# Threshold attention before two feed-forward layers: threshold sums per head on GpSimd, value products spread over five steps, a shorter warm-up

## The chip, the cores and the metric

The kernel runs on one core of a Trainium2 chip. The metric is the device time of one execution in microseconds (us). Engines are named as the profile names them: PE (TensorE) with its weight loads PEld, DVE (VectorE), ACT (ScalarE), POOL (GpSimd) and SP (SyncE, which issues DMAs).

## What is computed

Attention over 4 batches of 8 heads, 576 positions and 64 values per head, keeps of each row of scores only those within tau of the row's maximum; its output goes through a gated layer (width 1536) and a second one (width 2048), all in float32:

```
scores = scale * np.matmul(q, k.transpose(0, 1, 3, 2))
thresh = np.max(scores, axis=-1, keepdims=True) - tau
scores = np.where(scores >= thresh, scores, -1000000000.0)
scores = scores - np.max(scores, axis=-1, keepdims=True)
attn = np.exp(scores)
attn = attn / (np.sum(attn, axis=-1, keepdims=True) + 1e-09)
out = np.matmul(attn, v)
x = (sigmoid(x @ w_gate) * (x @ w_val)) @ w_out
x = g(x @ w_in) @ w_out2      # g: 0, a quarter parabola, then the identity
```

## The kernel before

Attention takes two heads (e = 0 and 1) at a time: 16 pairs p, each in five steps u = 0 to 4 of 128 rows of queries (step 4 holds the last 64 rows of both heads in one tile). The order is written by hand: `attention` counts t over 80 steps, and each engine takes what the steps issue to it strictly in that order. In step t:

- PE forms the scores of step t (`scores`, L235 and L239) in `wa` and `wb`, transposes the weights of step t-1 (`turns`, L280 and L281), and does a part of the products with the values (`attend`, L304), which `rounds` (L365) assigns to steps. A pair's products are cut into round 0 (query rows of steps 0 and 1) and round 1 (steps 2 to 4); each has five chunks c of keys, 0 to 3 from the tile `r`, 4 from the tile `rl`, with two products (one per head) for a chunk. Rounds of pair p run in steps 3, 4, 6 and 7 counted from its first; 5 and more lie in the next pair.
- DVE takes, head by head, the scaled negated scores and their row minimum (`maxima`, L248); POOL then adds tau for both heads in one instruction (L251); ACT takes the exponentials (`exponents`, L258); DVE multiplies by the mask and sums the rows (`masks`, L266, which reads the tiles `s` and `ex` and POOL's sum); POOL copies the rest of the keys (`lt`, L273).
- ACT copies the transposes of step t-1 from PSUM (`copies`, L286 to L296) and, when a round ends, its result (`drain`, L314).
- Once a pair, in step 0 of the next, DVE adds 1e-9 to the row sums and inverts them (`denom`, L318 and L319); they are transposed (L384), go to DRAM and back spread over the partitions (`sum_rows`, `spread`), and POOL multiplies the result by them in step 4 (`normalise`, L335).

Beside this, from step 12 on, a generator `background` puts one DVE or ACT operation of the conversion of the first weights behind the masks of a step, and later steps split the first inputs and weights of the next layer there. The feed-forward layers follow, bound by PE. Before the first scores, `warm` (L354) issues products of the identity with itself that no one reads.

Of the kernel before, what the change touches and what calls it, by code (L numbers as in the profile page):

```python
# [14 lines left out]
ALU = mybir.AluOpType  # L15
# [14 lines left out]
def kernel(  # L30
# [17 lines left out]
    nc = tc.nc  # L48
# [3 lines left out]
    NP, _, S = q.shape  # L52
# [7 lines left out]
    nf, R = divmod(S, P)  # L60
# [17 lines left out]
    tau_b = const.tile([P, 1], F32, name="tau_b")  # L78
# [8 lines left out]
    sums = [const.tile([P, 2 * nf + 1], F32, name=f"sum_{i}") for i in range(2)]  # L87
# [99 lines left out]
    def attention():  # L187
# [14 lines left out]
        U = nf + 1  # L202
# [8 lines left out]
        def load(p):  # L211
            t = qkp.tile([P, 2, S], F32, tag="qk", name="qk")
            nc.sync.dma_start(out=t[:, 0], in_=q[p])
            nc.sync.dma_start(out=t[:, 1], in_=k[p])
            qk[p] = t
# [9 lines left out]
        def corner(p):  # L225
            for e in range(2):
                es = slice(e * R, e * R + R)
                nc.gpsimd.tensor_copy(corners[p % 2][es, es], qk[p][es, 0, nf * P :])

        def scores(p, u):  # L230
            t = qk[p]
            for s in range(2):
                c = slice(s * HS, s * HS + HS)
                if u == nf:
                    nc.tensor.matmul(wa[:, s, :HS], corners[p % 2], t[:, 1, c], start=True, stop=True)  # L235
                    continue
                for e, w in enumerate((wa, wb)):
                    es = slice(e * D, e * D + D)
                    nc.tensor.matmul(  # L239
                        w[:, s, :HS], t[es, 0, u * P : u * P + P], t[es, 1, c], start=True, stop=True  # L240
                    )

        def maxima(p, u):

            t = sp.tile([P, 2, 2, HS], F32, tag="s", name="s")
            mx = mxs[u % 2]
            for e, w in enumerate((wa, wb)[: 1 if u == nf else 2]):
                nc.vector.tensor_scalar(  # L248
                    t[:, e], w[:, :, :HS], nscale, None, op0=ALU.mult, op1=ALU.min, accum_out=mx[:, 0, e : e + 1]
                )  # L250
            nc.gpsimd.tensor_scalar(mx[:, 1], mx[:, 0], tau_b, None, op0=ALU.add)  # L251
            st[p, u] = t, mx

        def exponents(p, u):
            t, mx = st[p, u]
            ex = pe_.tile([P, 2, 2, HS], F32, tag="ex", name="ex")
            for e in range(1 if u == nf else 2):
                nc.scalar.activation(ex[:, e], t[:, e], AF.Exp, scale=-1.0, bias=mx[:, 0, e : e + 1])  # L258
            st[p, u] = t, mx, ex

        def masks(p, u):
            t, mx, ex = st.pop((p, u))
            pr = pt[p, u] = pp.tile([P, 2, S], F32, tag="p", name="p")
            for e in range(1 if u == nf else 2):
                c = 2 * nf if u == nf else e * nf + u
                nc.vector.scalar_tensor_tensor(  # L266
                    pr[:, e], t[:, e].rearrange("p a b -> p (a b)"), mx[:, 1, e : e + 1],
                    ex[:, e].rearrange("p a b -> p (a b)"), op0=ALU.is_le, op1=ALU.mult,
                    accum_out=sums[p % 2][:, c : c + 1],
                )  # L270
            lt = lts[p, u] = pp.tile([P, 2, R], F32, tag="lt", name="lt")
            x = pr[:, :, nf * P :] if u < nf else pr[:, :1, nf * P :].broadcast_to((P, 2, R))
            nc.gpsimd.tensor_copy(lt, x)  # L273

        def turns(p, u):
            pr = pt.pop((p, u))
            for e in range(1 if u == nf else 2):
                for c in range(nf):
                    cs = slice(c * P, c * P + P)
                    nc.tensor.transpose(wt[:, e, cs], pr[:, e, cs], ident)  # L280
            nc.tensor.transpose(left[:, :P], lts.pop((p, u)).rearrange("p a b -> p (a b)"), ident)  # L281

        def copies(p, u):
            r, o = min(u // 2, 1), u % 2 * P if u < nf else 2 * P
            if u < nf:
                nc.scalar.activation(  # L286
                    rt[r].rearrange("p e c n -> p (e c) n")[:, :, o : o + P],
                    wt.rearrange("p e (c n) -> p (e c) n", n=P), AF.Copy,
                )
                nc.scalar.activation(rl[r][:, o : o + P], left[:, :P], AF.Copy)  # L290
                return
            for e in range(2):
                es = slice(e * R, e * R + R)
                x = wt[:, 0].rearrange("p (c n) -> p c n", n=P)
                nc.scalar.activation(rt[r][:, e, :, o : o + R], x[:, :, es], AF.Copy)
                nc.scalar.activation(rl[r][es, o : o + R], left[es, es], AF.Copy)  # L296

        def attend(p, r, cs):


            n = NR[r]
            for c in cs:
                for e in range(2):
                    nc.tensor.matmul(  # L304
                        av[e * D : e * D + D, :n], vs[p % 3][:, e, c], rt[r][:, e, c] if c < nf else rl[r],
                        start=c == 0, stop=c == nf,
                    )

        def x_of(p):
            b, hp = divmod(p, NHP)  # L310
            return xall[:, hp, b * S : (b + 1) * S]

        def drain(p, r):
            nc.scalar.activation(x_of(p)[:, r * NR[0] : r * NR[0] + NR[r]], av[:, : NR[r]], AF.Copy)  # L314

        def denom(p):
            rs = sums[p % 2]
            nc.vector.tensor_scalar(rs, rs, 1e-9, None, op0=ALU.add)  # L318
            nc.vector.reciprocal(rs, rs)  # L319

        def sum_rows(p):

            n = 2 * nf + 1
            nc.scalar.activation(rows[p % 2][:n], left[:n, P : 2 * P], AF.Copy)
            drs[p] = dram.tile([n, P], F32, tag="dr", name="dr")
            nc.sync.dma_start(out=drs[p], in_=rows[p % 2][:n])
# [24 lines left out]
        def warm(n):  # L351

            for _ in range(n):
                nc.tensor.matmul(av[:, :P], ident, ident, start=True, stop=True)  # L354
# [6 lines left out]
        load_v(1)  # L361
        for t in corners:
            nc.gpsimd.memset(t, 0.0)
        warm(30)
        corner(0)  # L365
        bg = background()

        rounds = {3: (0, 0, range(2)), 4: (0, 0, range(2, nf + 1)), 6: (0, 1, range(2)), 7: (0, 1, range(2, nf + 1))}
        parts = {}
        for p in range(NP):  # L370
            for i, (_, r, cs) in rounds.items():
                parts[p * U + i] = p, r, cs
        for t in range(N + 5):
            p, u = divmod(t, U)
            on = t < N
            at = divmod(t - 1, U) if 1 <= t <= N else None
            if on:
                scores(p, u)
            if t == N:
                yield t - N, True  # L380
            if at:
                turns(*at)
            if t % U == 1 and t > U:
                nc.tensor.transpose(left[: 2 * nf + 1, P : 2 * P], sums[(t // U - 1) % 2], ident)  # L384
            if t in parts:
                attend(*parts[t])
            if on:
                maxima(p, u)
                exponents(p, u)
            if at:  # L390
                copies(*at)
            if t % U == 1 and t > U:
                sum_rows(t // U - 1)
            if t in parts and parts[t][2][-1] == nf:
                drain(*parts[t][:2])
            if on:
                masks(p, u)
                if u == 1 and p + 1 < NP:
                    corner(p + 1)
                if u == 2 and p + 2 < NP:  # L400
                    load(p + 2)
                if u == 3 and p + 2 < NP:
                    load_v(p + 2)
            pd, ud = divmod(t - U, U)
            if ud == 0 and 0 <= pd < NP:
                denom(pd)
            if ud == 2 and 0 <= pd < NP:
                spread(pd)
            if ud == 4 and 0 <= pd < NP:
                normalise(pd)  # L410
            if 12 <= t < N:
                next(bg, None)
            if t == N - 1:
                run(bg)
                nc.scalar.activation(dummy, half, AF.Sigmoid)
                st1.close()
                wides[:] = [wb, wa, wt]
            if t == N + 2:
                st2.close()
                ps_o.close()  # L420
            yield t - N, False
# [258 lines left out]
```

## Time and profile before

| what | value |
|---|---|
| device time, median of 3 runs | 1195.66 us (1193.7 to 1196.68) |
| the profiled execution: its device time, its span | 1196.43 us, 1194.6 us |
| mean granted TensorE clock of the profiled execution | 0.992 |
| PE, PEld busy over the span | 1160.1 us (97%), 980.9 us (82%) |
| DVE, ACT, POOL busy over the span | 799.7 us (67%), 559.6 us (47%), 84.7 us (7%) |
| DMA | 122.31 MB, 102 GB/s |

The span runs from the first instruction to the last; the device time holds a little more. Busy times are sums over all stages, so a share says little about one stage; a matmul's end is modelled, and PE counts as busy where several short gaps lie between overlapping products. All sums in the prediction are made against the profiled execution and then moved to the median.

### The profile page before, as it was taken

The numbers are of one execution on the slowest core, as the hardware profiler recorded it, in microseconds if no ns is written. First come the engines' busy times: TensorE is split into PE (matmuls) and PEld (weight loads), VectorE is DVE, ScalarE is ACT, GpSimd is POOL, SyncE is SP. The second block draws the span as 40 slices with busy tenths as digits, with TensorE's granted clock in tenths as the row PEclk, the third lists the DMA queues.
The fourth block names the chain that finished last, engine by engine and source line by source line (L and its number), as shares of the span: only waits on it lengthen the run. The fifth ranks groups of instructions, "written<-read, shape, count | busy, mean of one in ns | idle before, by whom it ended". The sixth has DMA issues, their size and how long they took to land.

```text
span 1194.6 us, 17391 instructions
## 1 busy us (share of the span) xinstructions
PE 1160.1 (97%) x6556; PEld 980.9 (82%) x6556; DVE 799.7 (67%) x1507; ACT 559.6 (47%) x1027; POOL 84.7 (7%) x219
## 2 busy tenths in 40 slices
PE   8999999899989999999999999999999999999998
PEld 6555555555679999999999999999898989889897
DVE  4778888877678998956658564265556555575554
ACT  4666676766634444433334332253434444353433
POOL 1222222232200000000000000000000000000000
PEclk9989999999989999999999999999999999999999
DMA  3232323221245557533543533112120421132101
GB/s 89 61 95 66 108 61 78 60 61 45 93 173 196 200 169 238 202 129 136 185 153 113 184 115 124 36 54 71 53 71 1 176 69 55 36 137 75 54 18 53
DMA packets 59379, 122.31 MB, mean 102 GB/s; under 512 B 8976, under 2 KB 35232, under 8 KB 59296
## 3 DMA queue, kind: packets, MB, share of 16 engines
q1 hardware_dynamic: 59152, 121.20, 31.1%
q8 instruction: 52, 0.85, 0.3%
q14 instruction: 31, 0.25, 0.1%
q10 hardware_dynamic: 144, 0.00, 0.0%
HBM read 98.57 MB, written 22.62 MB: 101 GB/s over the span
## 4 chain that ended last, share of the span: by engine, by line
PE 76%; DVE 13%; ACT 4%; DMA 3%; issue 1%; POOL 1%; SPq 0%; POOLq 0%; ACTq 0%; DVEq 0%
PE w L537 17%; PE w L529 12%; PE pgv L446 8%; PE pgv L447 8%; PE pgv L448 8%; PE pu L448 6%; PE pu L447 6%; PE pu L446 6%; DVE s L248 5%; DVE p L266 5%; PE aw L304 2%; ACT ex L258 2%; PE w L239 2%; PE w L280 2%; DMA rb<-dr 2%
## 5 line engine op out<-in xcount | busy, mean ns | idle before, releaser
L446 PE MATMUL pgv<-xflat,ih 128*128 128x384 f32 x560 | 188.8, 337 | 6.1 <-ACT act L488 3.5
L447 PE MATMUL pgv<-xflat,ih 128*128 128x384 f32 x560 | 188.6, 337 | 0.0
L448 PE MATMUL pgv<-xflat,il 128*128 128x384 f32 x560 | 188.5, 337 | 0.0
L503 ACT ACTIVATE hh<-act 128x384 fp32r<-128x384 f32 x168 | 88.5, 527 | 180.8 <-DVE act L492 119.4
L258 ACT ACTIVATE ex<-s,mx 128x576 f32<-128x576 f32 x144 | 105.5, 773 | 106.4 <-DVE s L248 106.2
L266 DVE SCALAR_TENSOR_TENSOR p<-s,mx,ex 128x576 f32<-128x576 f32 x144 | 112.9, 817 | 47.5 <-POOL mx L251 28.7
L499 ACT ACTIVATE act<-act,half 128x384 f32<-128x384 f32 x96 | 59.2, 617 | 167.6 <-DVE act L496 167.6
L505 DVE TENSOR_TENSOR hl<-act,hh 128x384 fp32r<-128x384 f32 x168 | 94.8, 564 | 62.0 <-ACT hh L503 62.0
L448 PE MATMUL pu<-xflat,il 128*128 128x384 f32 x384 | 129.1, 336 | 0.0
L447 PE MATMUL pu<-xflat,ih 128*128 128x384 f32 x384 | 129.1, 336 | 0.0
L446 PE MATMUL pu<-xflat,ih 128*128 128x384 f32 x384 | 128.6, 335 | 0.0
L248 DVE TENSOR_SCALAR_CACHE_REDUCE s<-w,nscale 128x576 f32<-128x576 f32 x144 | 112.0, 811 | 20.9 <-PE w L239 20.9
L492 DVE TENSOR_TENSOR act<-pgv,act 128x384 f32<-128x384 f32 x70 | 38.9, 555 | 120.8 <-PE pgv L448 117.4
L537 PE MATMUL w<-oh,hh 128*128 128x512 f32 x288 | 114.0, 396 | 0.4 <-DVE xall L560 0.4
L537 PE MATMUL w<-oh,hl 128*128 128x512 f32 x288 | 114.1, 396 | 0.0
L537 PE MATMUL w<-ol,hh 128*128 128x512 f32 x288 | 114.1, 396 | 0.0
L446 PEld LDWEIGHTS pgv<-xflat,ih 128*128 128x128 f32 x560 | 105.9, 189 | 8.6 <-ACT act L488 4.1
L447 PEld LDWEIGHTS pgv<-xflat,ih 128*128 128x128 f32 x560 | 106.0, 189 | 1.8 <-DVE xflat L438 0.2
L280 PEld LDWEIGHTS w<-ident,p 128*128 128x128 f32 x576 | 62.0, 142 | 54.5 <-ACT r L286 28.7
L448 PEld LDWEIGHTS pgv<-xflat,il 128*128 128x128 f32 x560 | 106.0, 189 | 0.0
L280 PE MATMUL w<-ident,p 128*128 128x128 f32 x576 | 84.0, 284 | 17.4 <-ACT r L286 10.3
L500 DVE TENSOR_TENSOR act<-pu,act 128x384 f32<-128x384 f32 x96 | 53.5, 558 | 70.2 <-ACT act L499 70.2
(82 smaller groups left out, 2120.1 us busy)
## 6 DMA issues: line engine op xcount, KB each, us to landing
w<-saved SPq DMA_DIRECT2D x48, 512.0 KB
w<-saved SPq DMA_DIRECT2D x24, 768.0 KB
raw<-in_moe_w_out_dram SPq DMA_DIRECT2D x28, 512.0 KB
saved<-w SPq DMA_DIRECT2D x12, 768.0 KB
raw<-in_moe_w_in_dram SPq DMA_DIRECT2D x16, 512.0 KB
saved<-w SPq DMA_DIRECT2D x16, 512.0 KB
raw<-in_moe_w_gate_dram SPq DMA_DIRECT2D x12, 512.0 KB
raw<-in_moe_w_val_dram SPq DMA_DIRECT2D x12, 512.0 KB
```

The costliest lines, as they stand in the source:

```text
L248: nc.vector.tensor_scalar(t[:, e], w[:, :, :HS], nscale, None, op0=ALU.mult, op1=ALU.min, accum_out=mx[:, 0, e : e + 1])
L258: nc.scalar.activation(ex[:, e], t[:, e], AF.Exp, scale=-1.0, bias=mx[:, 0, e : e + 1])
L266: nc.vector.scalar_tensor_tensor(pr[:, e], t[:, e].rearrange("p a b -> p (a b)"), mx[:, 1, e : e + 1], ex[:, e].rearrange("p a b -> p (a b ...
L280: nc.tensor.transpose(wt[:, e, cs], pr[:, e, cs], ident)
L446: nc.tensor.matmul(ps, ih[:, i, kk], xh[:, kk, c], start=(kk == 0), stop=False)
L447: nc.tensor.matmul(ps, ih[:, i, kk], xl[:, kk, c], start=False, stop=False)
L448: nc.tensor.matmul(ps, il[:, i, kk], xh[:, kk, c], start=False, stop=(kk == KD - 1))
L499: nc.scalar.activation(act, act, AF.Square, scale=0.5, bias=half)
L503: nc.scalar.activation(hh[:, c], act, AF.Copy)
L505: nc.vector.tensor_tensor(hl_[:, c], act, f32(hh[:, c]), op=ALU.subtract)
L529: nc.tensor.matmul(at(y, a, b), l[:, ds_], r[:, c], start=new and m == 0, stop=last and m == 2, skip_group_check=True,)
L537: nc.tensor.matmul(y[i % 3][:, i // 3], l[:, ts_], r, start=first and m == 0, stop=last and m == 2,)
```

## The change

Four edits, all in `attention`. In `maxima`, POOL adds tau for each head right behind that head's maxima. The addition of 1e-9 leaves `denom` on DVE and becomes a POOL instruction in step 4 of the pair itself. `rounds` gives chunks 2 and 3 of round 0 to step 4 and its chunk 4, with the `drain` behind it, to step 5 (step 0 of the next pair); a step may now hold several parts. `warm` issues 10 products in place of 30.

```diff
@@ maxima
                 nc.vector.tensor_scalar(
                     t[:, e], w[:, :, :HS], nscale, None, op0=ALU.mult, op1=ALU.min, accum_out=mx[:, 0, e : e + 1]
                 )
-            nc.gpsimd.tensor_scalar(mx[:, 1], mx[:, 0], tau_b, None, op0=ALU.add)
+                nc.gpsimd.tensor_scalar(
+                    mx[:, 1, e : e + 1], mx[:, 0, e : e + 1], tau_b, None, op0=ALU.add
+                )
@@ denom
             rs = sums[p % 2]
-            nc.vector.tensor_scalar(rs, rs, 1e-9, None, op0=ALU.add)
             nc.vector.reciprocal(rs, rs)
@@ attention
-        warm(30)
+        warm(10)
...
-        rounds = {3: (0, 0, range(2)), 4: (0, 0, range(2, nf + 1)), 6: (0, 1, range(2)), 7: (0, 1, range(2, nf + 1))}
+        rounds = {3: (0, 0, 2), 4: (0, 2, 4), 5: (0, 4, 5), 6: (1, 0, 2), 7: (1, 2, 5)}
         parts = {}
         for p in range(NP):
-            for i, (_, r, cs) in rounds.items():
-                parts[p * U + i] = p, r, cs
+            for i, (r, a, b) in rounds.items():
+                parts.setdefault(p * U + i, []).append((p, r, range(a, b)))
...
-            if t in parts:
-                attend(*parts[t])
+            for part in parts.get(t, ()):
+                attend(*part)
...
-            if t in parts and parts[t][2][-1] == nf:
-                drain(*parts[t][:2])
+            for part in parts.get(t, ()):
+                if part[2][-1] == nf:
+                    drain(*part[:2])
...
             pd, ud = divmod(t - U, U)
+            if on and u == nf:
+                nc.gpsimd.tensor_scalar(sums[p % 2], sums[p % 2], 1e-9, None, op0=ALU.add)
             if ud == 0 and 0 <= pd < NP:
                 denom(pd)
```

On PE, from step 4 of a pair into step 0 of the next, before (`w_123` holds transposes, `w_121` and `w_122` the scores of the two heads, `aw` the products with the values):

```order
L304 MATMUL aw<-r_154,v_159 64x256 x4
L304 MATMUL aw<-rl_156,v_159 64x256 x2
L239 MATMUL w_121<-qk 128x288
L239 MATMUL w_122<-qk 128x288
L239 MATMUL w_121<-qk 128x288
L239 MATMUL w_122<-qk 128x288
L280 MATMUL w_123<-ident,p 128x128 x4
L281 MATMUL aw<-ident,lt 128x128
```

and the same place now:

```order
L306 MATMUL aw<-r_154,v_159 64x256 x4
L239 MATMUL w_121<-qk 128x288
L239 MATMUL w_122<-qk 128x288
L239 MATMUL w_121<-qk 128x288
L239 MATMUL w_122<-qk 128x288
L282 MATMUL w_123<-ident,p 128x128 x4
L283 MATMUL aw<-ident,lt 128x128
L306 MATMUL aw<-rl_156,v_159 64x256 x2
```

The two products with `rl` (chunk 4) stood ahead of the next pair's first scores and stand behind them and behind the transposes now.

On POOL, from step 3 of a pair to step 0 of the next, before:

```order
L251 TENSOR_SCALAR mx_84<-mx_84,tau_b 128x2
L273 COPY lt<-p 128x128
L251 TENSOR_SCALAR mx_83<-mx_83,tau_b 128x2
L273 COPY lt<-p 128x128
L335 TENSOR_TENSOR xall<-xall,rb_79 128x576
L251 TENSOR_SCALAR mx_83<-mx_83,tau_b 128x2
L273 COPY lt<-p 128x128
```

and now:

```order
L251 TENSOR_SCALAR mx_84<-mx_84,tau_b 128x1 x2
L275 COPY lt<-p 128x128
L251 TENSOR_SCALAR mx_83<-mx_83,tau_b 128x1
L275 COPY lt<-p 128x128
L408 TENSOR_SCALAR sum_88<-sum_88 128x9
L336 TENSOR_TENSOR xall<-xall,rb_79 128x576
L251 TENSOR_SCALAR mx_83<-mx_83,tau_b 128x1 x2
L275 COPY lt<-p 128x128
```

POOL has two additions of one column where it had one of two columns, and the addition to the row sums stands between the copy of step 4 and the multiplication of `normalise`.

## Rows read from the trace of the kernel before

**Rows 1.** Busy time by stage (us, share of the window; PEclk is the granted clock).

```profile
12.00:322.00 310.00, 287.77 (x1854) 172.38 (x1854) 247.62 (x648) 208.59 (x389) 79.45 (x203) 0.99 0.24 64
350.00:1195.00 845.00, 840.15 (x4520) 780.29 (x4519) 535.58 (x837) 336.19 (x609) 0.00 (x0) 1.00 0.32 111
```

**Rows 2.** Groups of instructions, DVE's two in attention, with the idle time before them.

```profile
L266 DVE SCALAR_TENSOR_TENSOR p<-s,mx,ex 128x576 f32<-128x576 f32 x144 | 112.9, 817 | 47.5 <-POOL mx L251 28.7 <-ACT ex L258 18.8
L248 DVE TENSOR_SCALAR_CACHE_REDUCE s<-w,nscale 128x576 f32<-128x576 f32 x144 | 112.0, 811 | 20.9 <-PE w L239 20.9
```

**Rows 3.** Timeline of DVE, step 4 of a pair to the next's step 1.

```profile
301.05 0.82 DVE L248 TENSOR_SCALAR_CACHE_REDUCE s<-w,nscale 128x576 f32<-128x576 f32 x1
...
302.85 0.82 DVE L266 SCALAR_TENSOR_TENSOR p<-s,mx,ex 128x576 f32<-128x576 f32 x1 [0.97 <-ACT ex L258]
...
304.77 0.82 DVE L248 TENSOR_SCALAR_CACHE_REDUCE s<-w,nscale 128x576 f32<-128x576 f32 x1 [1.10 <-PE w L239]
...
306.83 0.82 DVE L266 SCALAR_TENSOR_TENSOR p<-s,mx,ex 128x576 f32<-128x576 f32 x1 [0.49 <-POOL mx L251]
...
308.31 0.17 DVE L318 TENSOR_SCALAR sum<-sum 128x9 f32<-128x9 f32 x1
...
308.65 0.76 DVE L248 TENSOR_SCALAR_CACHE_REDUCE s<-w,nscale 128x576 f32<-128x576 f32 x1
```

**Rows 4.** The chain that ended last, from step 1 to step 3 of that pair.

```profile
309.51 1.45 ACT ex L258 x2
...
312.06 1.09 PE w L280 x8
...
313.27 1.77 PE aw L304 x12
315.03 1.22 PE w L239 x8
316.25 1.56 DVE s L248 x4
```

**Rows 5.** Timeline of PE in step 4, ahead of the next pair's scores.

```profile
302.97 0.60 PE L304 MATMUL aw<-rl,v 128*64 128x256 f32 x4
303.50 1.24 PE L239 MATMUL w<-qk 64*128 64x288 f32 x8
```

**Rows 6.** Timeline of POOL, and of DVE at its first row, in pair 5.

```profile
121.12 0.62 POOL L273 COPY lt<-p 128x128 f32<-128x128 f32 x1 [1.74 <-DVE p L266]
123.16 0.29 POOL L251 TENSOR_SCALAR mx<-mx,tau_b 128x2 f32<-128x2 f32 x1 [1.42 <-DVE s L248]
125.18 0.29 POOL L273 COPY lt<-p 128x128 f32<-128x128 f32 x1 [1.73 <-DVE p L266]
...
120.90 0.69 DVE L162 TENSOR_TENSOR w<-w,high 128x512 f32<-128x512 f32 x1
```

**Rows 7.** Timeline of the start, all engines.

```profile
0.72 0.39 SPq L213 DMA_DIRECT2D qk<-in_q_dram  x1
...
1.17 0.41 SPq L214 DMA_DIRECT2D qk<-in_k_dram  x1
...
1.34 9.07 PE L354 MATMUL aw<-ident 128*128 128x128 f32 x60 [1.34 <-POOL ident masks.py:199]
...
4.72 0.52 POOL L228 COPY corner<-qk 64x64 f32<-64x64 f32 x2 [2.70 <-DMA qk<-in_q_dram]
...
10.34 1.24 PE L239 MATMUL w<-qk 64*128 64x288 f32 x8
```

**Rows 8.** The warming products alone, in two stretches of 4 us.

```profile
1.40:5.40 4.00, 4.00 (x19) 4.00 (x20) 1.00 0.77 208
6.20:10.20 4.00, 4.00 (x38) 4.00 (x36) 1.00 0.89 271
```

**Rows 9.** The chain that ended last, where the first raw weights arrive.

```profile
59.26 10.14 DMA raw<-in_moe_w_gate_dram
```

**Rows 10.** Timeline of PE behind the last pair's step 4.

```profile
322.54 0.63 PE L280 MATMUL w<-ident,p 128*128 128x128 f32 x4 [0.32 <-DVE p L266]
```

## The prediction

> **What bounds the kernel now.** I read the stages first, then the groups with their waits, then one pair of attention in order of time. All four edits lie in attention, which takes some 310 us [rows 1]; in the 845 us behind it PE has almost no gap, and no instruction there is touched, so what attention saves arrives at the end whole or not at all. In attention no engine is full: PE 288 of 310 us, DVE 248, ACT 209 [rows 1]. The reader is to see what DVE waits for [rows 2]: its masks stand 28.7 us behind POOL's addition of tau and 18.8 us behind the exponentials, its maxima 20.9 us behind PE's scores. These waits are no sum of gains, because two loops run side by side. One is DVE alone: a step is two maxima and two masks, each 0.74 us from start to start, and the wait between. The other goes round through ACT and PE: maxima, exponentials, copy, transposes, products, scores, and the maxima two steps later [rows 4]; neither POOL nor a mask stands in it. Where it ends last, an earlier mask is worth nothing. One pair shows both. Its step 4 begins on DVE at 301.05, step 0 at 304.77 after a wait of 1.10 for PE's scores, step 1 at 308.65 [rows 3], step 3 at 316.25 [rows 4].
>
> **The change, part by part.** *Addition per head.* In a step of two heads the first mask starts 306.83 - 304.77 = 2.06 us after the first maxima and waits for POOL [rows 3]. In step 4, where POOL has one head only, it starts 302.85 - 301.05 = 1.80 us after, and the exponential is last. That 1.80 is what is late next in every step: POOL's sum for head 0 starts 0.74 us earlier and takes 0.29 [rows 6], and the exponential of head 0 does not move. Averaged over the 62 waits for POOL of the page the mask stands 28.7/62 = 0.46 us [rows 2]; two maxima end 2 x 0.74 + 0.08 = 1.56 after the start, so the new wait is about 0.24, and a step gains 0.22. Second masks start 0.74 behind the first, later than their own addition if that takes 0.29 too. Of the four such steps of a pair only step 0 is on DVE's loop alone: from step 1 to step 3 the way goes through ACT and PE (309.51 exponentials, then PE without a gap from 312.06 to 316.25 [rows 4]), from step 3 to step 0 it does so too, and 0 is taken for these. Bounds for a pair: 0.22 in one step, to 4 x 0.22 = 0.88.
>
> *The 1e-9.* DVE loses one instruction of 0.17 in step 0 [rows 3], on DVE's loop: 0.17 a pair. On POOL it adds about 0.29 (nearest row, the other addition [rows 6]) behind the copy of step 4 and ahead of the normalising product; DVE's reciprocal comes a whole step later and doesn't wait. What is queued behind it is the first addition of the next step 0, which has some 0.1 us to spare; that edge is in the range.
>
> *Products.* The four passes of chunk 4 take 303.50 - 302.97 = 0.53 us ahead of the next pair's first scores [rows 5], and DVE stands 1.10 for these scores [rows 3], so 0.53 a pair is saved there. They now follow the transposes of step 0, ahead of scores that wait for DVE to free their banks; there they are covered. With DVE sooner that cover shrinks; gone, it costs the 0.53 back. The drain moves along on ACT into step 0, behind that step's copies, and the next round begins after another set of transposes, so nothing waits for it. No DMA is moved past another; SP's order stays.
>
> *Sum over the pairs.* 0.22 + 0.17 + 0.53 = 0.92 us a pair. There are 15 intervals from pair to pair and most of a sixteenth, but the pair that waits 10.14 us for the first raw weights [rows 9] is paced by that transfer, and about one pair's gain goes there: 14.5 x 0.92 = 13.3 us. In pairs where conversions fill DVE the wait for scores is shorter and the masks count in more steps; I take the same sum for both.
>
> *Last pair.* Its chunk 4 used to lie ahead of a wait for DVE of 0.32 at 322.54 [rows 10] and now follows transposes with work behind them: 0.5 us lost.
>
> *Warm-up.* 30 products are 60 passes from 1.34 us on, and the first scores follow at 10.34 without a gap [rows 7]. The first stretch of 4 us holds 19 passes, the later one 38 [rows 8]: 0.21 us each, then 0.105, which is TensorE's lower level of 1.2 GHz and its upper one of 2.4 GHz; the clock column prints 1.00 for both, so at the start the pace tells the level. Ten products are 20 x 0.21 = 4.2 us, to 5.55. The data is there: q's load, issued at 0.72, was read at 4.72; k's, issued at 1.17, should land near 5.2 [rows 7]. So 10.34 - 5.55 = 4.8 us are gained at most; if the scores' 1.24 us run at the lower level they take as much again, 3.55; I take 4.1.
>
> The sum is -13.3 + 0.5 - 4.1 = -16.9 us. The profiled execution, 1196.43 us, lies 0.8 above the median of 1195.66; moved to the median the forecast is **1178.8 us**.
>
> At two places rows and rules differ. *The shared port.* POOL's copy of 0.29 us took 0.62 when DVE ran an operation with two SBUF inputs beside it, from 120.90 to 121.59 [rows 6]: it stood until that was done. The Trainium skill (SBUF — State Buffer, section "Who interferes with whom") says that such a DVE instruction and a GpSimd instruction that reads SBUF exclude each other, the one that issues first going first; the rows agree. A mask reads `s` and `ex`, both in SBUF, so by that rule the new addition for head 1, ready when the first mask starts, would lose the race or delay the mask; the sum with it is the first rival below. *The warm-up.* The Trainium skill (TensorE: Matmul & The Clock Gate, section "🔬 Part 1: The HAM clock gate (the "warmup" mystery)") has a slow clock as the default, released by activity; the two paces of the rows agree. By it, fewer warming products could leave the slow clock on; the sum by it is that of the third rival.
>
> **The rivals.** *The first mask shuts out POOL's second addition.* Before, the addition ran 1.7 us after the first maxima while DVE stood idle. Now the mask wants to start at 1.80, just as POOL begins. If the mask is first, POOL ends 0.15 after it (as the copy did: 121.74 against 121.59 [rows 6]), at 1.80 + 0.82 + 0.15 = 2.77, and the second mask starts at 2.80 in place of 2.06 + 0.74 = 2.80: the gain of the masks is gone. Then 0.17 + 0.53 are left in pairs where DVE stands for PE, and less, about 0.2, in the half where conversions fill DVE: some 14.5 x 0.45 = 6.5 us, in all -6.5 + 0.5 - 4.1 = -10.1, or 1185.6 us. For it: the rows of the copy. Against: the addition reads one column and may be through before the mask starts, and in half of the steps POOL starts 0.07 earlier than in the others. I give it 0.25.
>
> *DVE's loop is the bound in every step.* Then all four steps of two heads gain: 0.88 + 0.17 + 0.53 = 1.58 a pair, 22.9 in all, with the other two terms 26.5 us less: 1169.2 us. For it: the pairs with conversions; against: PE runs without a gap into the scores in steps 2 and 4 [rows 4, 5]. 0.08.
>
> *The clock stays low (slower).* If 20 passes don't raise it, the scores and transposes with their gaps must. At the lower level PE's part of two steps, 1.09 + 1.77 + 1.22 = 4.08 us [rows 4], doubles: 2.04 us more a step, where PE is on the way. It decides at 16.9 + 3.6 = 20.5 us, ten steps; if it lasted until the wait for raw weights, some 13 steps, it would be 26 us, and the time 1195.66 - 16.9 + 26 = 1204.8 us. Against: at the lower level PE would be busy nearly without a gap, which is what raised it before. 0.03.
>
> *Less of the front.* Low for two or three steps only, 5 us: 1184 us. 0.06.
>
> **How the numbers follow.** Forecast 0.58 (1174 to 1183, by the bounds of the warm-up and half of the masks' range), shut-out 0.25, DVE's loop 0.08, low clock briefly 0.06, long 0.03. The range, 1170.5 to 1187.5, holds the forecast, the brief low clock and the shut-out with the spread of 1.5 us of the runs, and leaves out the two far cases and the edges. About 0.3%, 3.6 us, is what a measurement of this kernel can tell from no change. All cases but the long low clock save more than that: faster 0.94; a shut-out that also costs the additions' time, near 1193, makes 0.03 for the same, and slower is 0.03.
>
> **What would show it.** In the new profile: first scores near 5.6; waits of the masks for POOL near zero and those for the exponentials up from 18.8 to about 30 us; the maxima's waits for scores not above 20.9, with step 0's smaller by half; from step 4 to the next step 3 in a pair without conversions 14.3 us in place of 316.25 - 301.05 = 15.2; POOL's one-column additions at 0.29. Additions of 0.9 us or more, or second masks that wait for POOL, mean the shut-out. Passes of 0.21 us behind 6 us mean the clock. The forecast is wrong if the pairs without conversions gain under 0.5 or over 1.4 us each.

## The result, and the profile after

The changed kernel took **1176.64 us**, median of 4 runs (1174.88 to 1177.82), beside 1196.17 (1193.7 to 1196.93) for the kernel before on the same chip: ratio 0.9839, interval 0.9819 to 0.9859, 19.3 us less. Savings against the kernel before are worked out in this way throughout: the ratio's distance from 1, times the median of the kernel before. The forecast was 1178.8 in a range of 1170.5 to 1187.5. The profiled run took 1174.88 us, with a span of 1173.1 us, 21.5 less than before's.

The groups of instructions of the changed kernel that answer to [rows 2], with the additions of one column and the new addition to the row sums:

```profile
L268 DVE SCALAR_TENSOR_TENSOR p<-s,mx,ex 128x576 f32<-128x576 f32 x144 | 112.9, 817 | 37.1 <-ACT ex L260 32.1 <-POOL mx L251 5.0
L248 DVE TENSOR_SCALAR_CACHE_REDUCE s<-w,nscale 128x576 f32<-128x576 f32 x144 | 112.1, 812 | 14.8 <-PE w L239 14.4
L251 POOL TENSOR_SCALAR mx<-mx,tau_b 128x1 f32<-128x1 f32 x144 | 40.7, 286 | 65.4 <-DVE s L248 64.8
L408 POOL TENSOR_SCALAR sum<-sum 128x9 f32<-128x9 f32 x16 | 4.5, 279 | 1.4
```

The masks' wait for POOL fell from 28.7 to 5.0 us and their wait for exponentials rose from 18.8 to 32.1: the next releaser took over most of it. All of the 5.0 us lie in steps 0, those of nine pairs; there POOL's normalising product (L336) can stand ahead of the additions, and the last experiments go after it. The maxima wait 14.4 us for scores in place of 20.9; 4.0 of that fall is the very first wait (6.48 us before, 2.50 now, below). An addition of one column takes 0.286 us, no less than one of two columns [rows 6].

DVE's timeline at the place of [rows 3], step 4 of pair 14 to step 3 of pair 15:

```profile
282.47 0.82 DVE L248 TENSOR_SCALAR_CACHE_REDUCE s<-w,nscale 128x576 f32<-128x576 f32 x1
...
285.90 0.82 DVE L248 TENSOR_SCALAR_CACHE_REDUCE s<-w,nscale 128x576 f32<-128x576 f32 x1 [0.81 <-PE w L239]
...
287.70 0.82 DVE L268 SCALAR_TENSOR_TENSOR p<-s,mx,ex 128x576 f32<-128x576 f32 x1 [0.23 <-POOL mx L251]
...
289.31 0.76 DVE L248 TENSOR_SCALAR_CACHE_REDUCE s<-w,nscale 128x576 f32<-128x576 f32 x1
...
292.71 0.82 DVE L248 TENSOR_SCALAR_CACHE_REDUCE s<-w,nscale 128x576 f32<-128x576 f32 x1
...
296.78 0.82 DVE L248 TENSOR_SCALAR_CACHE_REDUCE s<-w,nscale 128x576 f32<-128x576 f32 x1 [0.70 <-PE w L239]
```

The first mask stands 1.80 us behind the first maxima (2.06 before), and from 282.47 to 296.78 it is 14.31 us; the forecast said 14.3 in place of 15.2.

The start, all engines, for [rows 7]; first the row of the kernel before for DVE's first maxima:

```profile
11.62 0.82 DVE L248 TENSOR_SCALAR_CACHE_REDUCE s<-w,nscale 128x576 f32<-128x576 f32 x1 [6.48 <-PE w L239]
```

and the changed kernel:

```profile
1.34 4.63 PE L355 MATMUL aw<-ident 128*128 128x128 f32 x20 [1.34 <-POOL ident masks.py:199]
...
5.91 1.58 PE L239 MATMUL w<-qk 64*128 64x288 f32 x8
...
7.53 0.82 DVE L248 TENSOR_SCALAR_CACHE_REDUCE s<-w,nscale 128x576 f32<-128x576 f32 x1 [2.50 <-PE w L239]
```

The scores start at 5.91 in place of 10.34, and DVE's first maxima at 7.53 in place of 11.62: 4.09 us earlier. This start differs between kernels that have it in common: first maxima at 6.72 to 7.92 in the seven profiled here with ten warming products, at 11.62 to 12.06 in the four with thirty.

**Where the time went, by the traces.** The start of a pair is its first maxima on DVE. A row of the table adds up to the span; the last column holds pair 15 and all behind attention. The four kernels with one edit each are the first experiments below.

| kernel | to first maxima | pairs 0 to 2 and 14 | pairs 3 and 4 | pairs 5 to 13 | the rest |
|---|---|---|---|---|---|
| before | 11.62 | 73.96 | 42.09 | 177.10 | 889.83 |
| addition per head alone | 12.06 | 72.49 | 39.28 | 172.38 | 887.09 |
| 1e-9 alone | 11.87 | 73.40 | 42.08 | 175.14 | 889.41 |
| products alone | 11.77 | 72.14 | 40.93 | 174.50 | 889.46 |
| short warm-up alone | 7.46 | 73.98 | 41.08 | 177.45 | 888.83 |
| the change | 7.53 | 69.80 | 39.77 | 168.80 | 887.20 |

From one kernel to another, "pairs 3 and 4" and "the rest" move with the granted clock too. In pairs 5 to 13 it is 1.00 in four of the six; with 1e-9 alone and the short warm-up alone it is 0.91 and 0.92 in pair 11. Stretches of the kernel before, behind PE's wait in pair 3 and behind attention (columns as in [rows 1]):

```profile
70.00:78.00 8.00, 5.89 (x26) 3.60 (x26) 5.61 (x16) 5.17 (x12) 1.34 (x5) 0.57 0.13 35
...
343.00:354.00 11.00, 8.40 (x29) 7.61 (x28) 10.24 (x14) 2.81 (x6) 0.00 (x0) 0.53 0.69 221
```

and of the changed kernel:

```profile
64.00:68.00 4.00, 3.63 (x16) 2.42 (x18) 3.76 (x11) 3.01 (x7) 0.99 (x3) 0.58 0.00 1
...
324.00:328.00 4.00, 3.24 (x11) 2.73 (x9) 3.93 (x5) 0.00 (x0) 0.23 (x1) 0.57 0.27 84
```

TensorE was near its lower level for most of 19 us before and of 8 us now, at the same two places. The two spans differ by 2.2 us more than the ratio's 19.3; neither this excess nor pair 3's gain of 1.77 us can be put down to an edit.

### The profile page after: what moved, and what is told of

The parts are those of the page before. It is cut to its first block, busy times and chain, and to the rows that moved or that the text cites. A ratio compares the mean times of both kernels' runs of the same rounds, so it can differ in the third digit from the quotient of the medians.

```text
span 1173.1 us, 17441 instructions
## 1 busy us (share of the span) xinstructions
PE 1147.4 (98%) x6516; PEld 970.6 (83%) x6516; DVE 796.8 (68%) x1491; ACT 556.6 (47%) x1027; POOL 109.1 (9%) x299
## 4 chain that ended last, share of the span: by engine, by line
PE 78%; DVE 9%; ACT 6%; DMA 3%; issue 2%; POOL 1%; SPq 0%; ACTq 0%; DVEq 0%; POOLq 0%
PE w L541 17%; PE w L533 13%; PE pgv L450 8%; PE pgv L451 8%; PE pgv L452 8%; PE pu L452 6%; PE pu L451 6%; PE pu L450 6%; ACT ex L260 4%; DVE p L268 4%; DVE s L248 3%; PE aw L306 3%; PE w L239 2%; PE w L282 2%; DMA rb<-dr 2%
## 5 line engine op out<-in xcount | busy, mean ns | idle before, releaser
L268 DVE SCALAR_TENSOR_TENSOR p<-s,mx,ex 128x576 f32<-128x576 f32 x144 | 112.9, 817 | 37.1 <-ACT ex L260 32.1
L248 DVE TENSOR_SCALAR_CACHE_REDUCE s<-w,nscale 128x576 f32<-128x576 f32 x144 | 112.1, 812 | 14.8 <-PE w L239 14.4
L533 PE MATMUL w<-hl,oh 128*128 128x512 f32 (+1 forms) x288 | 97.1, 337 | 0.0
```

The lines of the kernel that those rows point to most:

```text
L248: nc.vector.tensor_scalar(t[:, e], w[:, :, :HS], nscale, None, op0=ALU.mult, op1=ALU.min, accum_out=mx[:, 0, e : e + 1])
L268: nc.vector.scalar_tensor_tensor(pr[:, e], t[:, e].rearrange("p a b -> p (a b)"), mx[:, 1, e : e + 1], ex[:, e].rearrange("p a b -> p (a b ...
L533: nc.tensor.matmul(at(y, a, b), l[:, ds_], r[:, c], start=new and m == 0, stop=last and m == 2, skip_group_check=True,)
```

## The experiments

**One edit at a time.** Each of the four edits of the diff was put alone into the kernel before. The intervals leave some 1.4 us on either side of each saving; by the medians the four would be 9.0, 3.1, 4.6 and 4.9 us.

*The addition per head alone.*

```diff
-            nc.gpsimd.tensor_scalar(mx[:, 1], mx[:, 0], tau_b, None, op0=ALU.add)
+                nc.gpsimd.tensor_scalar(
+                    mx[:, 1, e : e + 1], mx[:, 0, e : e + 1], tau_b, None, op0=ALU.add
+                )
```

> The kernel before with the addition per head alone. Theory of the forecast (each edit saves its own term): 0.22 us a pair in 14.5 pairs, 3.2 us less, ratio about 0.997; masks no longer wait for POOL (28.7 us of idle time before to under 8) and the waits of the maxima for scores stay near 20.9. Rival (the loop through ACT and PE holds the pair, so the earlier mask is given back): within 2 us of before, ratio 0.998 to 1.000, and the idle time taken from the masks comes back as waits of the maxima for PE's scores, 20.9 up to 26 us or more. Rival (shut-out by the shared port): masks wait as long as before, the additions take 0.6 us or more.

Measured: 1187.42 us, ratio 0.9939 (0.9926 to 0.9953), 7.3 us less: more than twice the forecast's term. Its groups on DVE:

```profile
L268 DVE SCALAR_TENSOR_TENSOR p<-s,mx,ex 128x576 f32<-128x576 f32 x144 | 112.9, 817 | 33.4 <-ACT ex L260 31.0 <-POOL mx L251 2.2 <-issue 0.2
L248 DVE TENSOR_SCALAR_CACHE_REDUCE s<-w,nscale 128x576 f32<-128x576 f32 x144 | 112.0, 811 | 25.0 <-PE w L239 24.6
```

The shut-out does not come about here: the masks' wait for POOL went from 28.7 to 2.2 us. Of the other two theories neither holds as it stands: the maxima's wait for scores rose from 20.9 to 24.6 us, as the first rival has it, and yet the time fell by more than either allows. The pairs show why. The lengths of the steps in pair 1, from first maxima to first maxima:

| kernel, pair 1 | 0 | 1 | 2 | 3 | 4 | pair |
|---|---|---|---|---|---|---|
| before | 3.87 | 3.40 | 4.18 | 3.47 | 3.73 | 18.65 |
| addition per head alone | 3.61 | 3.23 | 4.36 | 3.32 | 3.87 | 18.39 |
| 1e-9 alone | 3.67 | 3.41 | 4.18 | 3.47 | 3.72 | 18.45 |
| products alone | 3.87 | 3.41 | 4.04 | 3.46 | 3.29 | 18.07 |
| the change | 3.41 | 3.41 | 4.07 | 3.32 | 3.43 | 17.64 |

Without conversions, step 0 keeps its 0.26 us; what steps 1 and 3 gain (0.17 and 0.15) comes back as longer waits for scores in steps 2 and 4 (0.18 and 0.14). That is the forecast's picture and its 0.22. Pair 0, which has no products of an earlier pair on PE, gains 0.80. In pairs 5 to 13, where conversions fill DVE, more steps keep their gain: 4.72 us, 0.52 a pair.

*1e-9 on GpSimd alone*, the diff's two lines in `denom` and behind `pd, ud`.

> The kernel before with the addition of 1e-9 on GpSimd alone. Theory of the forecast: 0.17 us a pair, 2.5 us less, ratio 0.998. Rival (step 0 waits for PE's scores or the loop through ACT and PE holds): nothing, within 1 us. Rival (POOL's first sum of step 0 is pushed late by it): up to 0.2 us a pair more, 3 us slower, with the first mask of step 0 later than 2.06 us after its first maxima.

Measured: 1193.28 us, ratio 0.9974 (0.9963 to 0.9986), 3.1 us less. Step 0 is 0.20 shorter in pair 1, all others the same, and pairs 5 to 13 gain 0.22 each (0.28 without pair 11). The forecast's theory holds.

*Products spread alone*, the diff's lines on `rounds`, `parts`, `attend` and `drain`.

> The kernel before with the products spread alone. Theory of the forecast: 0.53 us a pair less the last pair's 0.5, 7.2 us less, ratio 0.994; step 0's wait of DVE for scores falls from 1.10 to about 0.57 and the step from step 4 to step 0 from 3.72 to about 3.2. Rival (the masks' loop on DVE with POOL in it now ends last in the steps behind, so that part of the gain is given back there): 3 to 5 us less, and steps 0 to 3 longer by some tenths of a us.

Measured: 1191.85 us, ratio 0.9967 (0.9957 to 0.9978), 3.9 us less, the rival's number, and in part its mechanism. In pair 1 step 4 loses 0.44 and step 2 another 0.14, 0.58 in all, and nothing is longer, as the forecast has it. Pairs 5 to 13 gain 2.60 together, 0.29 each, in place of 0.53. Two things take the rest. First, their steps 4 lose 3.00 us together, where 0.53 each would be 4.8: pair 6, for one, has a step 4 of 3.50 us in both kernels. DVE's timeline at its end, products alone:

```profile
145.12 0.69 DVE L162 TENSOR_TENSOR w<-w,high 128x512 f32<-128x512 f32 x1
145.72 0.81 DVE L248 TENSOR_SCALAR_CACHE_REDUCE s<-w,nscale 128x576 f32<-128x576 f32 x1
```

A conversion of 0.69 us fills what is a wait for scores in other pairs, and the maxima follow without one; in the kernel before it is the same. Second, their steps 0 grow by 0.46 us together. Pair 14, which has no conversions, shows how, with a step 0 of 4.18 us in place of 3.87. POOL and DVE there, before:

```profile
285.82 1.40 POOL L335 TENSOR_TENSOR xall<-xall,rb 128x576 f32<-128x576 f32 x1 [0.38 <-ACT xall L314]
286.13 0.82 DVE L248 TENSOR_SCALAR_CACHE_REDUCE s<-w,nscale 128x576 f32<-128x576 f32 x1 [1.10 <-PE w L239]
```

and with the products alone:

```profile
280.96 0.82 DVE L248 TENSOR_SCALAR_CACHE_REDUCE s<-w,nscale 128x576 f32<-128x576 f32 x1 [0.67 <-PE w L239]
281.62 1.41 POOL L335 TENSOR_TENSOR xall<-xall,rb 128x576 f32<-128x576 f32 x1 [0.89 <-DMA rb<-dr]
...
283.01 0.28 POOL L251 TENSOR_SCALAR mx<-mx,tau_b 128x2 f32<-128x2 f32 x1
283.32 0.82 DVE L266 SCALAR_TENSOR_TENSOR p<-s,mx,ex 128x576 f32<-128x576 f32 x1 [0.79 <-POOL mx L251]
```

POOL's normalising product, which waits for the row sums from DRAM, begins 0.66 us behind the step's first maxima in place of 0.31 ahead; the addition of tau stands behind it, and the first mask starts 2.36 us after the first maxima in place of 2.06. That is the rival's loop with POOL in it.

*Short warm-up alone*, `warm(10)` in place of `warm(30)`.

> The kernel before with 10 warming products in place of 30. Theory of the forecast: first scores near 5.6 to 5.9 in place of 10.34, 4.1 us less, ratio 0.9966, and the pairs as long as before. Rival (what is gained at the start goes into the wait for the first raw weights of the later stage, which a DMA paces): first maxima 4.1 us earlier, but less than 2 us left behind pair 4. Rival (clock): passes of 0.21 us behind 6 us and the gain gone.

Measured: 1191.49 us, ratio 0.9967 (0.9957 to 0.9977), 3.9 us less. First maxima at 7.46, and pairs 0 to 2 and 14 are 73.98 us together beside 73.96 before. The forecast's theory holds to within the scatter of the start; neither the load of the weights nor the clock took it back.

The four ratios make 7.3 + 3.1 + 3.9 + 3.9 = 18.2 us of the change's 19.3: in the time the edits add, within their intervals.

**Does a mask shut GpSimd out?** The prediction's first rival is tested by an addition that can't come before the mask.

```diff
-                nc.gpsimd.tensor_scalar(
-                    mx[:, 1, e : e + 1], mx[:, 0, e : e + 1], tau_b, None, op0=ALU.add
-                )
+                for _ in range(1 + e):
+                    nc.gpsimd.tensor_scalar(
+                        mx[:, 1, e : e + 1], mx[:, 0, e : e + 1], tau_b, None, op0=ALU.add
+                    )
```

> The changed kernel with GpSimd's addition for the second head issued twice, which leaves its result as it is. The second copy starts about 1.9 us after a step's first maxima, while the first mask (1.80 to 2.62, two operands in SBUF) runs. Theory (a one-column addition and the mask run beside each other): the copies take 0.29 us each, the second mask stays 0.74 behind the first, the time stays within 2 us of the changed kernel's 1176.6. Rival (the mask shuts GpSimd out, the rival of the prediction): the second copy ends about 0.15 us after the first mask, at 2.77, with a duration of 0.6 to 0.9 us, the second mask follows at 2.80 in place of 2.54, and a pair grows by up to 4 x 0.26 us, 5 to 15 us in all.

Measured: 1187.43 us, ratio to the kernel before 0.9934 (0.9918 to 0.9951), some 11 us slower than the changed kernel. A step of two heads, on DVE and POOL, with first maxima at 266.53:

```profile
266.53 0.81 DVE L248 TENSOR_SCALAR_CACHE_REDUCE s<-w,nscale 128x576 f32<-128x576 f32 x1
...
268.18 1.11 POOL L252 TENSOR_SCALAR mx<-mx,tau_b 128x1 f32<-128x1 f32 x2 [0.31 <-DVE s L248]
...
268.32 0.82 DVE L269 SCALAR_TENSOR_TENSOR p<-s,mx,ex 128x576 f32<-128x576 f32 x1 [0.23 <-ACT ex L261]
...
269.32 0.82 DVE L269 SCALAR_TENSOR_TENSOR p<-s,mx,ex 128x576 f32<-128x576 f32 x1 [0.18 <-POOL mx L252]
```

The rival's mechanism is there to the hundredth. The two additions for head 1 need 1.11 us; the second ends at 269.29, 0.15 behind the first mask's end at 269.14, and the second mask starts 2.79 behind the first maxima. In all 62 steps where the second addition begins beside the mask, it ends 0.15 behind it. It is not the longer queue alone: two additions of 0.28 with the 0.10 between them would be through at 2.31, ahead of a second mask at 2.54. The Trainium skill (SBUF — State Buffer, section "Who interferes with whom") has such a pair of instructions exclude each other, the first to issue going first; this trace agrees, for an addition of a single column too. The changed kernel escapes by little, here in a step of the same kind:

```profile
261.39 0.82 DVE L248 TENSOR_SCALAR_CACHE_REDUCE s<-w,nscale 128x576 f32<-128x576 f32 x1 [0.87 <-PE w L239]
...
263.05 0.28 POOL L251 TENSOR_SCALAR mx<-mx,tau_b 128x1 f32<-128x1 f32 x1 [0.45 <-DVE s L248]
...
263.19 0.82 DVE L268 SCALAR_TENSOR_TENSOR p<-s,mx,ex 128x576 f32<-128x576 f32 x1 [0.23 <-ACT ex L260]
```

Its addition for head 1 begins 0.14 us before the mask and takes its usual 0.28. The mask, which starts while the addition still runs, takes its usual 0.82, so in this order neither is seen to hold up the other.

**No warming products at all**, `warm(0)` in place of `warm(10)`.

> The changed kernel without any warming product. Theory (the granted clock rises only after a busy stretch, which the scores and transposes with their gaps give late): the first scores start with k's data near 5.2, run at passes of twice the length, and the clock is low for several steps: first maxima not before 8.2 us, pair 0 longer than 16.49 by up to 2 us a low step; 2 to 8 us slower than 1176.6. Rival (the scores raise the clock themselves within about a step): first maxima near 7.5 to 8.2, pair 0 within 1 us of 16.49, time within 1.5 us of 1176.6; then the ten products buy nothing.

Measured: 1177.54 us, ratio to the kernel before 0.9847 (0.9831 to 0.9862), no different from the changed kernel's 0.9839. PE's first passes:

```profile
5.51 2.29 PE L239 MATMUL w<-qk 64*128 64x288 f32 x8 [5.51 <-DMA qk<-in_k_dram]
8.68 3.02 PE L239 MATMUL w<-qk 64*128 64x288 f32 x8 [0.89 <-DVE s L248]
11.64 1.97 PE L282 MATMUL w<-ident,p 128*128 128x128 f32 x8
...
13.75 1.31 PE L239 MATMUL w<-qk 64*128 64x288 f32 x8
14.99 1.09 PE L282 MATMUL w<-ident,p 128*128 128x128 f32 x8
```

The theory is right that the clock stays low, for two steps: 2.29 us for the first eight passes of scores, which take 1.31 later, and 1.97 for the eight transposes that take 1.09 in the next step. (The pace tells the level, since the column of the granted clock prints 1.00 here as in [rows 8]; the second scores' 3.02 can hold waits for DVE too.) It is wrong on the price, where the rival's numbers came: pair 0 takes 17.33 us in place of 16.49, and the first maxima, at 7.80, lie within the scatter of the start. With the 0.27 between 7.80 and 7.53 that is 1.1 us at most. The rows show PE waiting there for k's data (to 5.51) and for DVE (0.89) besides. The Trainium skill (TensorE: Matmul & The Clock Gate, section "🔬 Part 1: The HAM clock gate (the "warmup" mystery)") has the slow clock as the default until activity releases it; the trace agrees.

**Conversions begun two steps later**, their loads as early as before. In the changed kernel ACT waits for these weights with the exponentials of pair 3 behind it:

```profile
61.69 0.66 ACT L138 ACTIVATE high<-raw 128x512 f32<-128x512 f32 x1 [2.78 <-DMA raw<-in_moe_w_gate_dram]
62.26 1.42 ACT L260 ACTIVATE ex<-s,mx 128x576 f32<-128x576 f32 x2
```

```diff
             yield
             yield
+            yield
+            yield
             for g in range(6):
                 extract(0, (g,), high0)
```

> The changed kernel with the conversion of the first weights begun two steps later, while their loads are issued as early as before. In the changed kernel ACT stands 2.78 us for these weights at the end of pair 2 with the exponentials of the next step behind it, pair 3 takes 20.99 us, and the granted clock is low for 3.4 us in it. Theory (this wait and the low clock that follows it are the whole excess of pair 3): pair 3 near 18.5 us, no low clock there, 2.5 us less, ratio 0.998. Rival (the conversions' end, now two steps later, runs into the next layer's work): pair 3 gains, but pairs 11 to 13 grow by as much.

Measured: 1174.93 us, ratio to the kernel before 0.9826 (0.9811 to 0.984); the step from 0.9839 is within the intervals. By the trace pair 3 takes 18.24 us in place of 20.99 with no low clock, but pairs 10 and 11 take 20.43 and 19.34 in place of 20.12 and 18.40. The theory holds for pair 3, with 2.7 us gained. Of the rival a part is seen: pairs 10 and 11 give back 1.25, but pairs 12 and 13 are as long as before.

**Products later still.**

```diff
-        rounds = {3: (0, 0, 2), 4: (0, 2, 4), 5: (0, 4, 5), 6: (1, 0, 2), 7: (1, 2, 5)}
+        rounds = {3: (0, 0, 2), 4: (0, 2, 3), 5: (0, 3, 5), 6: (1, 0, 3), 7: (1, 3, 5)}
```

> The changed kernel with one more chunk of round 0 moved from step 4 to step 0 of the next pair (0.53 us), and one of round 1 from step 2 to step 1 (0.66 us). Theory (step 4 is held by PE's scores, for which DVE still stands 0.81 us, step 2 likewise): the step from 4 to 0 falls from 3.43 to about 3.0 and step 2 from 4.07 to about 3.6 in pairs without conversions, 6 to 10 us less. Rival (the work moved stands ahead of the scores of steps 1 and 2 now and is given back there): steps 0 and 1 grow by 0.3 to 0.6, less than 2 us gained.

Measured: 1178.24 us, ratio to the kernel before 0.9848 (0.9828 to 0.9869), no gain. The profile also has pair 3 at 23.3 us in place of 21.0, with more low clock, so single pairs say more than its sum. In pair 14 step 4 fell from 3.43 to 3.00 as the theory has it. Steps 1 and 2 traded evenly (3.32 and 4.13 became 3.86 and 3.53), and step 0 grew from 3.54 to 3.94. The rival put that on PE; DVE and POOL in this step say otherwise:

```profile
268.81 0.82 DVE L248 TENSOR_SCALAR_CACHE_REDUCE s<-w,nscale 128x576 f32<-128x576 f32 x1 [0.38 <-PE w L239]
...
269.43 1.41 POOL L336 TENSOR_TENSOR xall<-xall,rb 128x576 f32<-128x576 f32 x1 [0.24 <-DMA rb<-dr]
...
270.83 0.53 POOL L251 TENSOR_SCALAR mx<-mx,tau_b 128x1 f32<-128x1 f32 x2
271.14 0.82 DVE L268 SCALAR_TENSOR_TENSOR p<-s,mx,ex 128x576 f32<-128x576 f32 x1 [0.77 <-POOL mx L251]
```

The normalising product starts when its row sums land, the additions stand behind it, and the mask starts 2.33 us after the first maxima. Pair 1, where no such product exists yet, has a step 0 of 3.40.

**The same with the normalising product in halves**, the second half two steps into the next pair.

```diff
-        def normalise(p):
-            nc.gpsimd.tensor_tensor(x_of(p), x_of(p), rbs[p % 2], op=ALU.mult)
+        def normalise(p, a, b):
+            x = x_of(p)[:, a:b]
+            nc.gpsimd.tensor_tensor(x, x, rbs[p % 2][:, a:b], op=ALU.mult)
...
             if ud == 4 and 0 <= pd < NP:
-                normalise(pd)
+                normalise(pd, 0, S if pd >= NP - 2 else S // 2)
+            if ud == 2 and 0 <= pd - 1 < NP - 2:
+                normalise(pd - 1, S // 2, S)
```

> The kernel of products_later_still with GpSimd's normalising product cut into halves: one stays in step 4, the other moves behind the copy of step 2 of the next pair. In products_later_still the first mask of step 0 starts 2.33 us after its first maxima, since the two additions wait for the normalising product (1.41 us, begun when its row sums land). Theory (this is where that kernel's gain in step 4 was given back): with 0.7 us left there the mask starts at 1.80 again, step 0 is back at 3.40 from 3.84 to 3.94 while the step from 4 to 0 stays at 3.00; clean pairs 17.2 us, the fifteen pairs 5 to 6 us shorter than the changed kernel's. Rival (step 0 is long because its products stand ahead of the scores of step 1): step 0 stays above 3.8 and the time near 1178.

Measured: 1168.76 us, ratio to the kernel before 0.9774 (0.9758 to 0.9791). The same step:

```profile
262.21 0.82 DVE L248 TENSOR_SCALAR_CACHE_REDUCE s<-w,nscale 128x576 f32<-128x576 f32 x1 [0.38 <-PE w L239]
...
262.68 0.80 POOL L337 TENSOR_TENSOR xall<-xall,rb 128x288 f32<-128x288 f32 x1
...
263.45 0.69 POOL L251 TENSOR_SCALAR mx<-mx,tau_b 128x1 f32<-128x1 f32 x2
...
264.00 0.82 DVE L268 SCALAR_TENSOR_TENSOR p<-s,mx,ex 128x576 f32<-128x576 f32 x1 [0.23 <-ACT ex L260]
```

The mask is back at 1.79, step 0 at 3.40, pair 14 at 17.20 us (17.75 in the changed kernel), and the fifteen pairs take 271.49 us in place of 278.37. The steps 0 of pairs 5 to 13 take 34.39 us together, beside 37.86 in the changed kernel and 40.74 with the whole product. The theory holds; the rival falls.

**All together**: this kernel, with the conversions begun one step later (one more `yield`).

> As later_and_halves, and the conversions begun one step later (the load's wait on ACT in the changed kernel was 2.78 us, a step is 3.3 us). Theory: the gains add, about 5.5 us by the halves and the products and 2 by pair 3, which takes 18.2 us with no low clock in it: near 1169, ratio to the kernel before 0.977. Rival (shorter pairs push the first weights' arrival or the work at the end of attention together): pairs 3, 10 and 11 grow back, 1172 or more.

Measured: **1165.69 us**, ratio to the kernel before 0.9745 (0.973 to 0.976), the fastest version here, some 11 us below the changed kernel, and below the 1169 that was expected: pair 3 takes 17.71 us with the clock at its upper level, where the profile of the kernel without the shift has 22.7. Pairs 10 and 11 did not grow together as the rival feared: 19.37 and 18.38 us beside 19.91 and 18.20.

## Why the prediction was right, and where not

- *The number*: 16.9 us less forecast, 19.3 measured. In the stretches with the same granted clock (the start, pairs 0 to 2 and 4 to 14) the traces show 17.1 us, and the forecast has 4.1 + 14 x 0.92 = 17.0 for them. That the two are so close is partly luck, as the terms show.
- *What bounds attention*: right in the main. Two loops, of which only one ends last in a step, are seen in the addition alone: where scores end last, an earlier mask comes back as a wait for scores. What was missed is POOL's normalising product in step 0. Of the 20.9 us that the maxima wait for scores, 6.5 are the wait at the very start and no part of the pairs.
- *Addition per head*: the mechanism and the 0.22 for pairs without conversions are right (0.26 measured). The step that failed is "I take the same sum for both": in pairs 5 to 13 the addition is worth 0.52 (and 0.80 in pair 0), and the edit 7.3 us in place of 3.2.
- *Products*: 0.53 forecast, 0.58 measured in pair 1. The same sentence failed here the other way: 0.29 in pairs 5 to 13, by conversions that fill the wait and by the normalising product on POOL, and 3.9 us in place of 7.2. That the two errors cancel is luck. In the change as a whole pairs 5 to 13 gain 8.30 us, 0.92 each, which was the forecast's number for a pair, and pair 1 gains 1.01.
- *1e-9*: 0.17 forecast, 0.20 measured. The edge that was named, the first addition of step 0 with "some 0.1 us to spare", does show in the changed kernel, and larger: the spare time had no row behind it, and before, the normalising product of pair 14's step 0 ended 1.09 us after the first maxima (285.82 + 1.40 beside 286.13), when an addition per head is ready at 0.99. In the changed kernel pair 14's step 0 is 3.54 us and pair 1's 3.41. In pairs 4 to 12 the first mask of step 0 starts 1.98 to 2.53 us after the first maxima, and 1.79 to 2.03 with the product in halves. With the products alone it is late in pair 14 too, so shorter steps are enough for it, without the 1e-9.
- *Step 0's wait for scores* was to halve from 1.10; it is 0.81. DVE comes sooner as well: step 3 is 0.15 shorter (3.32 in place of 3.47), and with the products alone, where it isn't, the wait is 0.67.
- *Warm-up*: 4.1 forecast, 4.09 measured. The closeness is luck: 4.1 was taken between bounds of 3.55 and 4.8, and the start scatters by more than a microsecond. The scores began 4.43 us sooner, not 4.8, and took 0.34 longer (1.58 in place of 1.24), not up to 1.24.
- *Last pair*: 0.5 us lost was forecast. From its step 4 on the change is 1.9 us shorter, but the clock was low there for less time, and with the products alone no loss shows either (from step 4 on 874.6 us beside 874.9, with some less low clock). Whether it exists is open.
- *The rivals*: the shut-out is a real mechanism, avoided by 0.14 us; with the second addition doubled it cost some 11 us, where the rival was priced at 6.8 above the forecast. The low clock was overpriced: without any warming it costs 1.1 us at most, not 26. DVE's loop as the bound in every step is not borne out: pairs without conversions gained 0.26 from the addition where that rival has 0.88, and pairs with conversions 0.52.

## What to carry to other kernels

Before a wait's whole size is booked as a gain, ask for each kind of stage which loop ends last there; an average wait hides that, and one edit alone in the old kernel shows it step by step. Where an operation on GpSimd must run beside a DVE operation with two SBUF operands, start it first: here a lead of 0.14 us parted the changed kernel from one 11 us slower. When an edit shortens one step and the time doesn't move, look at what is queued ahead of the next short instruction on a lightly loaded engine: here a 1.41 us product on POOL, an engine busy for 7% of the span before, had eaten the gain.

## What was not expected of the hardware

- The scatter of a kernel's runs goes largely with the granted clock: the five runs of the addition alone have spans of 1183.3 to 1187.5 us at mean clocks of 0.999 to 0.994. It isn't all of it: at 0.994 the kernel before has spans from 1191.9 to 1195.4. In pair 3, behind PE's wait, the kernel with the addition alone kept the upper level where the kernel before fell:

```profile
69.00:77.00 8.00, 5.80 (x44) 3.83 (x45) 7.17 (x21) 5.49 (x13) 2.13 (x8) 1.00 0.08 16
```

  Its pair 3 took 20.18 us and the kernel before's 22.76. Differences of 2 us between single profiles of this kernel are therefore no evidence on an edit unless the clock's rows are compared too.
- GpSimd's addition takes 0.29 us for one column as for two [rows 6], so splitting it costs POOL a whole instruction. POOL, busy for 7% of the span before, had the time for it in all steps but step 0.
